# Maxout as (a+b)/2 + |a−b|/2 in a fused attention and maxout kernel

**Chip, cores, metric.** One core of one Trainium2 chip. Times are device microseconds (us) of one execution, as medians of several runs; the span of a profile is the time from the first to the last instruction of the one profiled execution, some 2 us less.

## The reference

Eight batches of block-causal attention (8 heads, 576 positions, head size 64, blocks of 64), whose output is x with 4608 tokens of 512, and then a maxout layer:

```python
attn_out = softmax(masked(q k^T / 8)) v          # per batch and head
x  = attn_out.transpose(0, 2, 1, 3).reshape(4608, 512)
h1 = x @ w1                                      # 512 x 1024
h2 = x @ w2
g  = maximum(h1, h2)
out = g @ w_out                                  # 1024 x 512
```

## The kernel before

The program is one list of instructions in an order chosen by hand: attention goes two head pairs at a time, and matmuls of the maxout layer ("units", one `yield` for each matmul) fill the gaps that attention leaves on TensorE. `fill(n)` takes such matmuls to the worth of n of 512 columns (one of 256 columns counts half). The transposed x lies whole in one SBUF tile, `xT`. The parts that matter:

```python
xT = ring.tile([P, NDM, NTOK + BLK], BF16, name="xT")
w1_sb = wpool.tile([P, NDM, d_ff], BF16, name="w1_sb")
w2_sb = wpool.tile([P, NDM, d_ff], BF16, name="w2_sb")
...
def load_w(f0, fw, which=(0, 1)):            # fp32 in HBM, bf16 in SBUF: the DMA casts
    for i in which:
        dst, src = ((w1_sb, w1r), (w2_sb, w2r))[i]
        nc.gpsimd.dma_start(out=dst[:, :, f0:f0 + fw], in_=src[:, :, f0:f0 + fw])
...
def h_unit(i, f):                            # 128 columns of h, up to 512 tokens
    ...
    for w_sb in (w1_sb, w2_sb):
        pt = ps_m.tile([P, SPAN], FP32, name="ps_h", tag="m")
        for c in range(NDM):                 # NDM = 4
            nc.tensor.matmul(pt[:, :w], w_sb[:, c, ...], xT[:, c, t0:t0 + w], ...)
            if c == NDM - 1:
                if not ph:
                    nc.vector.tensor_copy(out=h1[:, :w], in_=pt[:, :w])
                else:
                    nc.vector.tensor_max(g[:, f, m:m + w], h1[:, :w], pt[:, :w])
                ...
            yield

def y_unit(i, s):                            # 128 tokens of the output
    for f in range(NFF):                     # NFF = 8
        nc.tensor.matmul(py[:], g[:, f, ...], wo_sb[:, f, :], ...)
        ...

def x_out(g, t0=0, t1=NCH, copies=(dve, dve)):   # context -> transposed x
    ...                                          # transposes on TensorE into pe, po
    copies[0](out=dst[:, :, :, 0], in_=pe[:])    # dst is a part of xT
    copies[1](out=dst[:, :, :n_odd, 1], in_=po[:])
```

The start of the schedule (cut): the first two pairs' scores, then `av(0, [0, 1])`, and so on to `x_out(0, 0, 2, (act, act))`, which writes the first piece of xT with ACT, then `x_out(1, 0, 2)` with VectorE, then the first `fill(2)`. The masks of the attention weights (`masks_q`), the loads of v and the casts of q and k are GpSimd's, in program order.

The softmax here doesn't subtract the row's maximum and nothing guards it: scores larger than these inputs give would overflow.

Of the kernel before, what the change touches and what calls it, by code (L numbers as in the profile page):

```python
# [8 lines left out]
FP32 = mybir.dt.float32  # L9
BF16 = mybir.dt.bfloat16  # L10
# [4 lines left out]
def kernel(  # L15
# [10 lines left out]
    nc = tc.nc  # L26

    B, H, S, D = q.shape
    P = 128
# [3 lines left out]
    d_model = H * D  # L33
    d_ff = moe_w1.shape[1]
    NDM = d_model // P
    NFF = d_ff // P
    NTOK = B * S
# [44 lines left out]
    xpool = ctx.enter_context(tc.tile_pool(name="xp", bufs=3))  # L82
    raw = ctx.enter_context(tc.tile_pool(name="raw", bufs=4))
    qkn = ctx.enter_context(tc.tile_pool(name="qkn", bufs=2))
    h1_pool = ctx.enter_context(tc.tile_pool(name="h1", bufs=3))
    g_pool = ctx.enter_context(tc.tile_pool(name="g", bufs=2))
    y_pool = ctx.enter_context(tc.tile_pool(name="y", bufs=4))
    ps_s = ctx.enter_context(tc.tile_pool(name="ps_s", bufs=2, space=bass.MemoryType.PSUM))
# [9 lines left out]
    vv_r = [ring.tile([P, NCH, H, D + 1], BF16, name=f"vv{r}") for r in range(NV)]  # L98
    aT_r = [ring.tile([P, 2, AW + APAD], BF16, name=f"aT{r}") for r in range(NA)]
    xT = ring.tile([P, NDM, NTOK + BLK], BF16, name="xT")  # L100
    w1_sb = wpool.tile([P, NDM, d_ff], BF16, name="w1_sb")
    w2_sb = wpool.tile([P, NDM, d_ff], BF16, name="w2_sb")
    wo_sb = wpool.tile([P, NFF, d_model], BF16, name="wo_sb")
    ident = wpool.tile([P, P], BF16, name="ident")

# [35 lines left out]
    w2r = moe_w2.rearrange("(c p) f -> p c f", p=P)  # L141
    wor = moe_w_out.rearrange("(c p) f -> p c f", p=P)

    def load_w(f0, fw, which=(0, 1)):
        for i in which:
            dst, src = ((w1_sb, w1r), (w2_sb, w2r))[i]
            nc.gpsimd.dma_start(out=dst[:, :, f0:f0 + fw], in_=src[:, :, f0:f0 + fw])

    def load_wo(c0, n):
        nc.gpsimd.dma_start(out=wo_sb[:, c0:c0 + n, :], in_=wor[:, c0:c0 + n, :])  # L150
# [11 lines left out]
    load_qk(2, (SP, None))  # L162
    make_identity(nc, ident)
    for r in range(NV):
        nc.vector.memset(vv_r[r][:, :, :, D:D + 1], 1.0)
        nc.vector.memset(vv_r[r][:BLK, NCH - 1, :, :], 0.0)
    for r in range(NA):
        nc.vector.memset(aT_r[r][:, :, AW:], 0.0)
# [3 lines left out]
    cast("k", 0, ((act, 0, 5), (dve, 5, RPP)))  # L172
    for c in range(2):
        load_v(0, c)
    load_w(0, 256, (0,))
    cast("q", 1, ((pool, 7, RPP),))
    cast("k", 1, ((pool, 0, 7),))
    load_w(0, 256, (1,))
    load_qk(2, (None, SP), gated=True)


    done_tokens = [0]
    g_tiles = {}

    def h_unit(i, f):
        if f == 0:
            g_tiles[i] = g_pool.tile([P, NFF, SPAN + BLK], BF16, name="g")
            if carry[i]:
                end = carry[i - 1] + spans[i - 1][1]
                nc.gpsimd.tensor_copy(  # L190
                    out=g_tiles[i][:, :, :carry[i]],
                    in_=g_tiles[i - 1][:, :, end - carry[i]:end])
        g = g_tiles[i]
        t0, w = spans[i]
        m = carry[i]
        ph = []
        for w_sb in (w1_sb, w2_sb):
            pt = ps_m.tile([P, SPAN], FP32, name="ps_h", tag="m")
            for c in range(NDM):
                nc.tensor.matmul(  # L200
                    pt[:, :w], w_sb[:, c, f * P:(f + 1) * P], xT[:, c, t0:t0 + w],
                    start=(c == 0), stop=(c == NDM - 1),
                )
                if c == NDM - 1:
                    if not ph:
                        h1 = h1_pool.tile([P, SPAN], BF16, name="h1")
                        nc.vector.tensor_copy(out=h1[:, :w], in_=pt[:, :w])  # L207
                    else:
                        nc.vector.tensor_max(g[:, f, m:m + w], h1[:, :w], pt[:, :w])  # L209
                    ph.append(pt)  # L210
                yield

    def y_unit(i, s):
        g = g_tiles[i]
        t0 = spans[i][0] - carry[i] + s * P
        py = ps_m.tile([P, d_model], FP32, name="ps_y", tag="m")
        for f in range(NFF):
            nc.tensor.matmul(  # L218
                py[:], g[:, f, s * P:(s + 1) * P], wo_sb[:, f, :],
                start=(f == 0), stop=(f == NFF - 1),  # L220
            )
            if f == NFF - 1:
                y = y_pool.tile([P, d_model], FP32, name="y")
                (dve if i < 2 else act)(out=y[:], in_=py[:])  # L224
                nc.sync.dma_start(out=out[t0:t0 + P, :], in_=y[:])
            yield

    def y_last(i, s):
        g = g_tiles[i]
        t0 = spans[i][0] - carry[i] + s * P  # L230
        for m, w, copy, queue in ((0, 256, act, SP), (256, P, dve, SP), (384, P, act, ACT)):
            py = ps_m.tile([P, w], FP32, name="ps_y", tag="m")
            for f in range(NFF):
                nc.tensor.matmul(  # L234
                    py[:], g[:, f, s * P:(s + 1) * P], wo_sb[:, f, m:m + w],
                    start=(f == 0), stop=(f == NFF - 1),
                )
                if f == NFF - 1:
                    y = y_pool.tile([P, w], FP32, name="yl")
                    copy(out=y[:], in_=py[:])  # L240
                    queue.dma_start(out=out[t0:t0 + P, m:m + w], in_=y[:])
                yield


    units = []

    def plan():
        def h(i, f):
            t0, w = spans[i]
            units.append((h_unit(i, f), t0 + w, w / SPAN, 2 * NDM))  # L250

        def y(i, s, last=False):
            t0, w = spans[i]
            if last:
                units.append((y_last(i, s), t0 + w, 0.333, 3 * NFF))
            else:
                units.append((y_unit(i, s), t0 + w, 1.0, NFF))

        for i in range(NSPAN):
            for f in range(NFF):  # L260
                h(i, f)
                if i > 2 and f % 2 == 0 and f // 2 < tiles[i - 1]:
                    y(i - 1, f // 2)
            if i == 1:
                for j in range(2):
                    for s in range(tiles[j]):
                        y(j, s)
        n = tiles[-1]
        for s in range(n):
            y(NSPAN - 1, s, s == n - 1)  # L270
# [13 lines left out]
    def fill(n):  # L284
        while n > 0 and at[0] < len(steps) and steps[at[0]][1] <= done_tokens[0]:
            u, _, cost = steps[at[0]]
            next(u)
            n -= cost
            at[0] += 1
# [74 lines left out]
    def burst_p(p):  # L364
        burst(p, ((0, 0, QCUT), (1, P, QCUT - P)), 0)
# [4 lines left out]
    def burst_q2(p):  # L370
        burst(p, ((1, 448, P), (2, QCUT, 320), (4, 512, BLK)), 896)
# [8 lines left out]
    def masks_q(p, eng=None):  # L380
        for a in (1024, 1408):
            mask(p, a, eng)
# [34 lines left out]
    def av(p, ts):  # L417
        b, hp = divmod(p, HP)
        vv = vv_r[b % NV]
        a = aT_r[p % NA]  # L420
        n = len(ts)
        h0 = hp // 2 * 4 + hp % 2
        if p % 2 == 0 and ts[0] == 0:
            xps[p // 2] = xpool.tile([P, NCH, 2, 2, D], BF16, name="xp")
        xp = xps[p // 2]
        po = ps_m.tile([P, n, 2, D + 1], FP32, name="ps_o", tag="m")
        n_mm = 2 * sum(t + 1 for t in ts)
        mm = 0
        for gi, t in enumerate(ts):
            for hh in range(2):  # L430
                for c in range(t + 1):
                    a0 = a_col(p, c, t)
                    nc.tensor.matmul(  # L433
                        po[:, gi, hh, :], a[:, hh, a0:a0 + P], vv[:, c, h0 + 2 * hh, :],
                        start=(mm == 0), stop=(mm == n_mm - 1),
                    )
                    mm += 1
        rec = small.tile([P, 3, 2, 1], FP32, name="rec")
        nc.vector.reciprocal(rec[:, :n, :, 0], po[:, :, :, D])  # L439
        nc.vector.tensor_mul(  # L440
            xp[:, ts[0]:ts[0] + n, :, p % 2], po[:, :, :, :D],
            rec[:, :n].to_broadcast([P, n, 2, D]),
        )
# [26 lines left out]

    def fill_of(g):
        if g == NG - 1:
            return 54
        left = 5 - g if g < 5 else 2 - (g - 5) % 2
        return -(-max(0, ready() - KEEP) // left)

# [44 lines left out]
    masks_p(1)  # L521
    for c in range(2, NCH):
        load_v(0, c)
    load_w(256, 256)
    cq = transposes("q", 1, (dve, dve))
    burst_q1(0)
    ck = transposes("k", 1, (dve, dve))
# [2 lines left out]
        ck((i,), LOW)  # L530
    cq((0,), HIGH, act)
    cq((1,), HIGH, act)
    load_w(512, 512)
    warm_up(3)
    burst_p(2)
    ck((0,), HIGH, dve)
# [1 line left out]
    av(0, [0, 1])  # L538
    warm_up(2)
    burst_p(3)  # L540
    av(1, [0, 1])
    masks_p(2, nc.vector)
    burst_q3(0)
    masks_p(3, nc.vector)
    burst_q2(0)
    av(2, [0, 1])
    warm_up(2)
    x_out(0, 0, 2, (act, act))
# [8 lines left out]
    warm_up(2)  # L557
    burst_q3(1)
    masks_q(1)
    for c in range(3):  # L560
        load_v(1, c)
    fill(2)
    load_qk(3, (SP, SP), gated=True)
    burst_q1(2)
    transposes("q", 2, (dve, act))()
    fill(3)
    burst_q2(2)
    av(0, [2, 3, 4])
    fill(1)
    burst_q3(2)  # L570
    masks_q(2)
    for c in range(3, NCH):
# [14 lines left out]
    cast("q", 3, ((pool, 0, RPP),))  # L587
    cast("k", 3, ((pool, 0, RPP),))
    load_qk(4, (SP, SP), gated=True)
    load_wo(0, 4)  # L590
    load_wo(4, 4)
    fill(3)

    x_due = []
# [35 lines left out]
    for p in range(NPAIR - LAG, NPAIR):  # L630
        if x_due:
            x_out(x_due.pop())
        av_with(p, 5)
        fill(11)
    x_out(NG - 1)
    fill(len(steps))

# [35 lines left out]
```

## Time and profile before

| | before |
|---|---|
| time, median of the 4 runs beside the result (range) | 282.98 us (282.7 to 285.0) |
| span of the profiled run, mean granted clock | 281.0 us, 1.00 |
| TensorE busy | 96% |
| steady part: time for two head pairs and 256 tokens of maxout | 15.0 us |

The page's slices of the span (40 of 7.0 us, busy tenths of TensorE, then its granted clock in tenths) show no hole:

```profile
PE   8699999999999999999999999999999999999995
...
PEclk9999999999999999999999999999999999999999
```

The evictions of h that the change touches, from the groups by form (count, busy us, mean ns):

```profile
L207 DVE CAST h<-ps_h 128x512 bf16<-128x512 f32 x56 | 38.7, 691 | 20.1 <-PE ps_h L200 18.4
L209 DVE TENSOR_TENSOR g<-h,ps_h 128x512 bf16<-128x512 bf16 x56 | 38.4, 686 | 9.1 <-PE ps_h L200 9.1
```

Both kinds of eviction cost the same, and VectorE waits for TensorE in front of them, not the other way round. (The trace of before lacks some 45 matmul records: 3208 matmuls against 3253 weight loads in the busy line below, so TensorE's sums of before are a little low.)

### The profile page before, as it was taken

How to read it: one execution, taken by the hardware profiler on the slowest of the kernel's cores; microseconds unless marked ns; L12 is line 12 of the kernel's file. 1: busy time of each engine (PE TensorE's matmuls, PEld its weight loads, DVE VectorE, ACT ScalarE, POOL GpSimd, SP SyncE). 2: the span in 40 equal slices, each digit the busy share in tenths (PEclk: the TensorE clock that was granted, in tenths of full speed). 3: DMA queues.
4: the chain of work that ended last, by engine and by line, in shares of the span. 5: the costliest groups of instructions: out<-in, count | busy, mean ns of one | idle time of the engine just before them, and what ended most of it. 6: DMA issues, size and time to landing. Idle time of an engine off the chain costs nothing.

```text
span 281.0 us, 7771 instructions
## 1 busy us (share of the span) xinstructions
PE 269.6 (96%) x3208; PEld 151.4 (54%) x3253; DVE 185.1 (66%) x387; ACT 140.8 (50%) x198; POOL 108.3 (39%) x272
## 2 busy tenths in 40 slices
PE   8699999999999999999999999999999999999995
PEld 2356767655556455555555554646454644444543
DVE  5867779668887666767767676757655766455530
ACT  3796577667565565555648375564653000100112
POOL 2996456764754625254343715372120000000000
PEclk9999999999999999999999999999999999999999
DMA  7999999989924993579266875175301111011114
GB/s 259 265 222 224 177 230 274 251 136 203 214 25 160 141 181 63 193 77 244 49 208 70 213 86 184 62 79 45 66 14 40 51 59 42 37 75 40 72 41 149
DMA packets 55940, 36.68 MB, mean 131 GB/s; under 512 B 38752, under 2 KB 43232, under 8 KB 55904
## 3 DMA queue, kind: packets, MB, share of 16 engines
q0 software_dynamic: 41728, 7.87, 34.7%
q1 hardware_dynamic: 13760, 27.66, 29.0%
q10 hardware_dynamic: 416, 0.66, 0.7%
q8 instruction: 25, 0.41, 0.6%
q14 instruction: 11, 0.09, 0.1%
HBM read 34.60 MB, written 9.44 MB: 157 GB/s over the span
## 4 chain that ended last, share of the span: by engine, by line
PE 94%; DVE 2%; ACT 2%; issue 2%; ACTq 0%
PE ps_h L200 43%; PE ps_y L218 22%; PE ps_o L433 11%; PE ps_s L325 8%; PE ps_w L295 3%; PE ps_qT L306 2%; PE ps_xe L455 2%; PE ps_kT L306 2%; ACT aT L349 1%; PE ps_s L343 1%; PE ps_y L234 1%; DVE kT L314 0%; DVE g L209 0%; DVE qn L131 0%; PE ps_xo L457 0%
## 5 line engine op out<-in xcount | busy, mean ns | idle before, releaser
L200 PE MATMUL ps_h<-xT,w_sb 128*128 128x512 bf16 (+3 forms) x605 | 136.2, 357 | 1.7 <-issue 0.3
L349 ACT ACTIVATE aT<-ps_s 128x1024 bf16<-128x1024 f32 (+2 forms) x100 | 96.1, 996 | 16.6 <-PE ps_s L325 15.5
L200 PEld LDWEIGHTS <-w_sb 128*128 128x128 bf16 x640 | 57.8, 98 | 57.4 <-issue 8.1
L207 DVE CAST h<-ps_h 128x512 bf16<-128x512 f32 (+3 forms) x80 | 51.0, 637 | 29.0 <-PE ps_h L200 26.6
L218 PE MATMUL ps_y<-wo_sb,g 128*128 128x512 bf16 x273 | 65.5, 379 | 2.1 <-PE ps_s L325 1.3
L354 POOL MEMSET aT<- 64x128 bf16 x124 | 22.5, 200 | 93.2 <-ACT aT L349 91.7
L209 DVE TENSOR_TENSOR g<-h,ps_h 128x512 bf16<-128x512 bf16 (+3 forms) x80 | 50.6, 632 | 11.8 <-PE ps_h L200 10.1
L224 ACT COPY y<-ps_y 128x512 f32<-128x512 f32 x31 | 18.1, 585 | 70.3 <-PE ps_y L218 56.5
L433 PEld LDWEIGHTS <-aT 128*128 128x128 bf16 x960 | 37.2, 98 | 13.5 <-issue 0.8
L218 PEld LDWEIGHTS <-g 128*128 128x128 bf16 x280 | 26.7, 98 | 30.4 <-issue 1.1
L433 PE MATMUL ps_o<-vv,aT 128*128 128x65 bf16 x960 | 39.8, 194 | 0.0
L135 POOL DMA_DIRECT2D vv<-in_v_dram x40 | 33.7, 847 | 0.5
L325 PE MATMUL ps_s<-qT,kT 64*128 64x64 bf16 (+6 forms) x344 | 31.6, 279 | 1.6 <-ACT kT L314 0.7
L440 DVE TENSOR_TENSOR xp<-ps_o,rec 128x256 bf16<-128x256 f32 (+1 forms) x64 | 31.4, 491 | 2.2
L439 DVE RECIPROCAL rec<-ps_o 128x4 f32<-128x4 f32 (+1 forms) x64 | 12.0, 188 | 21.6 <-PE ps_o L433 20.0
L314 ACT COPY qT<-ps_qT 128x576 bf16<-128x576 bf16 (+1 forms) x17 | 10.3, 614 | 29.4 <-PE ps_qT L306 29.4
L190 POOL COPY g<-g 128x512 bf16<-128x512 bf16 x8 | 4.9, 613 | 38.3 <-DVE g L209 38.2
L131 POOL CAST qn<-qraw 128x1152 bf16<-128x1152 f32 (+1 forms) x16 | 16.9, 1058 | 6.4 <-DMA qraw<-in_q_dram 6.3
L131 POOL CAST kn<-kraw 128x1152 bf16<-128x1152 f32 (+1 forms) x15 | 17.1, 1140 | 5.1 <-DMA kraw<-in_k_dram 2.6
L460 DVE COPY xT<-ps_xe 128x640 bf16<-128x640 bf16 (+2 forms) x17 | 7.9, 463 | 16.1 <-PE ps_xe L455 14.9
L314 ACT COPY kT<-ps_kT 128x576 bf16<-128x576 bf16 x15 | 9.6, 638 | 15.0 <-PE ps_kT L306 15.0
L325 PEld LDWEIGHTS <-kT 64*128 64x128 bf16 x344 | 13.2, 95 | 6.8 <-issue 3.0
(46 smaller groups left out, 145.5 us busy)
## 6 DMA issues: line engine op xcount, KB each, us to landing
qraw<-in_q_dram SPq DMA_DIRECT2D x16, 576.0 KB, 4.1
out_dram<-y SPq DMA_DIRECT2D x35, 256.0 KB, 2.1
kraw<-in_k_dram SPq DMA_DIRECT2D x15, 576.0 KB, 5.5
vv<-in_v_dram POOLq DMA_DIRECT2D x32, 128.0 KB, 5.4
w_sb<-in_moe_w_dram POOLq DMA_DIRECT2D x4, 256.0 KB, 6.5
w_sb<-in_moe_w_dram POOLq DMA_DIRECT2D x2, 512.0 KB, 10.9
wo_sb<-in_moe_w_out_dram POOLq DMA_DIRECT2D x2, 512.0 KB, 11.9
kraw<-in_k_dram ACTq DMA_DIRECT2D x1, 576.0 KB, 5.4
```

What stands on the lines that cost most here:

```text
L131: copy(out=n[:, j0:j1], in_=t[:, j0:j1])
L135: nc.gpsimd.dma_start(out=vv_r[b % NV][P - rows:, c, :, :D], in_=v[b, :, c * P:c * P + rows, :].rearrange("h p d -> p h d"),)
L200: nc.tensor.matmul(pt[:, :w], w_sb[:, c, f * P:(f + 1) * P], xT[:, c, t0:t0 + w], start=(c == 0), stop=(c == NDM - 1),)
L207: nc.vector.tensor_copy(out=h1[:, :w], in_=pt[:, :w])
L209: nc.vector.tensor_max(g[:, f, m:m + w], h1[:, :w], pt[:, :w])
L218: nc.tensor.matmul(py[:], g[:, f, s * P:(s + 1) * P], wo_sb[:, f, :], start=(f == 0), stop=(f == NFF - 1),)
L314: (copy or copies[i])(out=t[:, p0 * RPP:p1 * RPP].rearrange("q (p j) -> q p j", j=RPP), in_=pts[i][:, :, p0:p1].rearrange("q j p -> q p j"),)
L325: nc.tensor.matmul(ps[:, hh, col:col + w], kT[r, k0:k0 + P], qT[r, q0:q0 + w], start=True, stop=True,)
L349: nc.scalar.activation(out=aT_r[p % NA][:, :, a0:a0 + w], in_=ps[:, :, :w], func=AF.Exp, scale=scale,)
L354: (eng or nc.gpsimd).memset(aT_r[p % NA][BLK:, :, a0:a0 + BLK], 0.0)
L433: nc.tensor.matmul(po[:, gi, hh, :], a[:, hh, a0:a0 + P], vv[:, c, h0 + 2 * hh, :], start=(mm == 0), stop=(mm == n_mm - 1),)
L440: nc.vector.tensor_mul(xp[:, ts[0]:ts[0] + n, :, p % 2], po[:, :, :, :D], rec[:, :n].to_broadcast([P, n, 2, D]),)
```

## The change

max(a, b) = (a+b)/2 + |a−b|/2, so out = ½ [ |x(w1−w2)| w_out + x ((w1+w2) w_out) ]. One h product instead of two, with |·| as its eviction; M = (w1+w2) w_out is made once; each output tile takes four more matmuls, x M. The ½ goes into attention's normalisation (the ones column of v becomes 2). To form w1−w2 and w1+w2 in fp32, w1 and w2 are now loaded as fp32 in four chunks of 256 columns, through four slots in the part of xT that is written last; the sum is written beside them.

```diff
-    w1_sb = wpool.tile([P, NDM, d_ff], BF16, name="w1_sb")
-    w2_sb = wpool.tile([P, NDM, d_ff], BF16, name="w2_sb")
+    d_sb = wpool.tile([P, NDM, d_ff], BF16, name="d_sb")
+    sT_sb = wpool.tile([P, NFF, d_model], BF16, name="sT_sb")
+    m_sb = wpool.tile([P, NDM, d_model], BF16, name="m_sb")
...
+    spare = xT[:, :, NTOK - 8 * WB - d_ff:NTOK]
+    w_slots = [spare[:, :, n * 2 * WB:(n + 1) * 2 * WB].bitcast(FP32) for n in range(4)]
+    s_sb = spare[:, :, 8 * WB:8 * WB + d_ff]
...
+    def load_w(j, which=(0, 1)):
+        for i in which:
+            w_raws[j, i] = t = w_slots[2 * (j % 2) + i]
+            nc.gpsimd.dma_start(out=t, in_=(w1r, w2r)[i][:, :, j * WB:(j + 1) * WB])
+    def combine_w(j):
+        fs = slice(j * WB, (j + 1) * WB)
+        nc.vector.tensor_sub(d_sb[:, :, fs], w_raws[j, 0], w_raws[j, 1])
+        nc.gpsimd.tensor_add(s_sb[:, :, fs], w_raws[j, 0], w_raws[j, 1])
...
-        nc.vector.memset(vv_r[r][:, :, :, D:D + 1], 1.0)
+        nc.vector.memset(vv_r[r][:, :, :, D:D + 1], 2.0)
...  h_unit: one product, evicted by
+        nc.vector.tensor_reduce(out=out, in_=in_.unsqueeze(2), op=max, axis=X,
+            apply_absolute_value=True)
...  new units: 32 transposes of s_sb into sT_sb, and M = sT_sb x wo_sb (32 matmuls)
...  y_unit: four terms (xT, m_sb) ahead of the eight (g, wo_sb)
...  schedule of the start: combine_w(0), load_w(2) after burst_p(3); combine_w(1), load_w(3)
...  before av(2, [0, 1]); combine_w(2) after masks_q(1); combine_w(3) after av(0, [2, 3, 4]);
...  load_wo behind load_w(3); the first fillers fill(2), fill(3), fill(1) become 4, 4 and 2
```

More of the change, by code (lines that the diff above doesn't have):

```diff
@@ L84 @@
     qkn = ctx.enter_context(tc.tile_pool(name="qkn", bufs=2))
-    h1_pool = ctx.enter_context(tc.tile_pool(name="h1", bufs=3))
     g_pool = ctx.enter_context(tc.tile_pool(name="g", bufs=2))
@@ L142 @@
     wor = moe_w_out.rearrange("(c p) f -> p c f", p=P)
-    def load_w(f0, fw, which=(0, 1)):
-        for i in which:
-            dst, src = ((w1_sb, w1r), (w2_sb, w2r))[i]
-            nc.gpsimd.dma_start(out=dst[:, :, f0:f0 + fw], in_=src[:, :, f0:f0 + fw])
+    WB = 256
+    w_raws = {}
+    spare = xT[:, :, NTOK - 8 * WB - d_ff:NTOK]
+    w_slots = [spare[:, :, n * 2 * WB:(n + 1) * 2 * WB].bitcast(FP32) for n in range(4)]
+    s_sb = spare[:, :, 8 * WB:8 * WB + d_ff]
+    def load_w(j, which=(0, 1)):
+        for i in which:
+            w_raws[j, i] = t = w_slots[2 * (j % 2) + i]
[4 more added lines that the diff above has]
+        nc.gpsimd.tensor_add(s_sb[:, :, fs], w_raws[j, 0], w_raws[j, 1])
     def load_wo(c0, n):
@@ L174 @@
         load_v(0, c)
-    load_w(0, 256, (0,))
+    load_w(0, (0,))
     cast("q", 1, ((pool, 7, RPP),))
     cast("k", 1, ((pool, 0, 7),))
-    load_w(0, 256, (1,))
+    load_w(0, (1,))
     load_qk(2, (None, SP), gated=True)
@@ L183, with ABS @@
     g_tiles = {}
+    def ABS(out, in_):
+        nc.vector.tensor_reduce(
+            out=out, in_=in_.unsqueeze(2), op=mybir.AluOpType.max,
+            axis=mybir.AxisListType.X, apply_absolute_value=True)
     def h_unit(i, f):
@@ L195, in h_unit, with sT_unit, m_unit @@
         m = carry[i]
-        ph = []
-        for w_sb in (w1_sb, w2_sb):
-            pt = ps_m.tile([P, SPAN], FP32, name="ps_h", tag="m")
-            for c in range(NDM):
-                nc.tensor.matmul(
-                    pt[:, :w], w_sb[:, c, f * P:(f + 1) * P], xT[:, c, t0:t0 + w],
-                    start=(c == 0), stop=(c == NDM - 1),
-                )
-                if c == NDM - 1:
-                    if not ph:
-                        h1 = h1_pool.tile([P, SPAN], BF16, name="h1")
-                        nc.vector.tensor_copy(out=h1[:, :w], in_=pt[:, :w])
-                    else:
-                        nc.vector.tensor_max(g[:, f, m:m + w], h1[:, :w], pt[:, :w])
-                    ph.append(pt)
+        pt = ps_m.tile([P, SPAN], FP32, name="ps_h", tag="m")
+        for c in range(NDM):
+            nc.tensor.matmul(
+                pt[:, :w], d_sb[:, c, f * P:(f + 1) * P], xT[:, c, t0:t0 + w],
+                start=(c == 0), stop=(c == NDM - 1),
+            )
+            if c == NDM - 1:
+                ABS(g[:, f, m:m + w], pt[:, :w])
+            yield
+    def sT_unit(j):
+        pt = ps_m.tile([P, 2, NDM, P], BF16, name="ps_sT", tag="m")
+        for i in range(2):
+            f = 2 * j + i
+            for c in range(NDM):
+                nc.tensor.transpose(pt[:, i, c, :], s_sb[:, c, f * P:(f + 1) * P], ident[:])
+                if i == 1 and c == NDM - 1:
+                    (dve if j % 2 else act)(
+                        out=sT_sb[:, 2 * j:2 * j + 2, :],
+                        in_=pt.rearrange("p i c d -> p i (c d)"))
                 yield
-    def y_unit(i, s):
-        g = g_tiles[i]
-        t0 = spans[i][0] - carry[i] + s * P
-        py = ps_m.tile([P, d_model], FP32, name="ps_y", tag="m")
+    def m_unit(c):
+        pt = ps_m.tile([P, d_model], FP32, name="ps_M", tag="m")
         for f in range(NFF):
             nc.tensor.matmul(
-                py[:], g[:, f, s * P:(s + 1) * P], wo_sb[:, f, :],
+                pt[:], sT_sb[:, f, c * P:(c + 1) * P], wo_sb[:, f, :],
                 start=(f == 0), stop=(f == NFF - 1),
@@ L222, in y_unit, with y_terms @@
             if f == NFF - 1:
+                (act, dve)[c % 2](out=m_sb[:, c, :], in_=pt[:])
+            yield
+    def y_terms(i, s):
+        g = g_tiles[i]
+        t0 = spans[i][0] - carry[i] + s * P
+        return [(xT[:, c, t0:t0 + P], m_sb[:, c]) for c in range(NDM)] + [
+            (g[:, f, s * P:(s + 1) * P], wo_sb[:, f]) for f in range(NFF)]
+    def y_unit(i, s):
+        t0 = spans[i][0] - carry[i] + s * P
+        py = ps_m.tile([P, d_model], FP32, name="ps_y", tag="m")
+        terms = y_terms(i, s)
+        for n, (lhs, rhs) in enumerate(terms):
+            nc.tensor.matmul(
+                py[:], lhs, rhs, start=(n == 0), stop=(n == len(terms) - 1),
+            )
+            if n == len(terms) - 1:
                 y = y_pool.tile([P, d_model], FP32, name="y")
@@ L228, in y_last @@
     def y_last(i, s):
-        g = g_tiles[i]
         t0 = spans[i][0] - carry[i] + s * P
@@ L232, in y_last @@
             py = ps_m.tile([P, w], FP32, name="ps_y", tag="m")
-            for f in range(NFF):
+            terms = y_terms(i, s)
+            for n, (lhs, rhs) in enumerate(terms):
                 nc.tensor.matmul(
-                    py[:], g[:, f, s * P:(s + 1) * P], wo_sb[:, f, m:m + w],
-                    start=(f == 0), stop=(f == NFF - 1),
+                    py[:], lhs, rhs[:, m:m + w], start=(n == 0), stop=(n == len(terms) - 1),
                 )
-                if f == NFF - 1:
+                if n == len(terms) - 1:
                     y = y_pool.tile([P, w], FP32, name="yl")
@@ L245 @@
     units = []
+    NY = NDM + NFF
     def plan():
@@ L249, in h @@
             t0, w = spans[i]
-            units.append((h_unit(i, f), t0 + w, w / SPAN, 2 * NDM))
+            units.append((h_unit(i, f), t0 + w, w / SPAN, NDM))
         def y(i, s, last=False):
@@ L254, in y @@
             if last:
-                units.append((y_last(i, s), t0 + w, 0.333, 3 * NFF))
+                units.append((y_last(i, s), t0 + w, 0.333, 3 * NY))
             else:
-                units.append((y_unit(i, s), t0 + w, 1.0, NFF))
+                units.append((y_unit(i, s), t0 + w, 1.0, NY))
         for i in range(NSPAN):
@@ L261, in plan @@
                 h(i, f)
+                if i == 0 and f % 2 == 1:
+                    units.append((sT_unit(f // 2), 0, 0.3, 2 * NDM))
                 if i > 2 and f % 2 == 0 and f // 2 < tiles[i - 1]:
@@ L264, in plan @@
             if i == 1:
+                for c in range(NDM):
+                    units.append((m_unit(c), 0, 1.0, NFF))
                 for j in range(2):
@@ L472, in fill_of @@
         if g == NG - 1:
-            return 54
+            return 45
         left = 5 - g if g < 5 else 2 - (g - 5) % 2
@@ L523 @@
         load_v(0, c)
-    load_w(256, 256)
+    load_w(1)
     cq = transposes("q", 1, (dve, dve))
@@ L532 @@
     cq((1,), HIGH, act)
-    load_w(512, 512)
     warm_up(3)
@@ L540 @@
     burst_p(3)
+    combine_w(0)
+    load_w(2)
     av(1, [0, 1])
@@ L545 @@
     burst_q2(0)
+    combine_w(1)
+    load_w(3)
+    load_wo(0, 4)
+    load_wo(4, 4)
     av(2, [0, 1])
@@ L559 @@
     masks_q(1)
+    combine_w(2)
     for c in range(3):
         load_v(1, c)
-    fill(2)
+    fill(4)
     load_qk(3, (SP, SP), gated=True)
@@ L565 @@
     transposes("q", 2, (dve, act))()
-    fill(3)
+    fill(4)
     burst_q2(2)
     av(0, [2, 3, 4])
-    fill(1)
+    combine_w(3)
+    fill(2)
     burst_q3(2)
@@ L589 @@
     load_qk(4, (SP, SP), gated=True)
-    load_wo(0, 4)
-    load_wo(4, 4)
     fill(3)
@@ L633 @@
         av_with(p, 5)
-        fill(11)
+        fill(9)
     x_out(NG - 1)
```

## The prediction

> **What bounds the kernel now.** I read the page's busy line first, then the chain that ended last, then the windows of the steady part, then the timeline of the first 30 us.
>
> ```profile
> PE 269.6 (96%) x3208; PEld 151.4 (54%) x3253; DVE 185.1 (66%) x387; ACT 140.8 (50%) x198; POOL 108.3 (39%) x272
> ...
> PE 94%; DVE 2%; ACT 2%; issue 2%; ACTq 0%
> PE ps_h L200 43%; PE ps_y L218 22%; PE ps_o L433 11%; PE ps_s L325 8%; PE ps_w L295 3%; PE ps_qT L306 2%; PE ps_xe L455 2%; PE ps_kT L306 2%; ACT aT L349 1%; PE ps_s L343 1%; PE ps_y L234 1%; DVE kT L314 0%; DVE g L209 0%; DVE qn L131 0%; PE ps_xo L457 0%
> ```
>
> The span is 281.0 us (the quoted time of 282.94 is about 1.9 above it). TensorE is busy 96% of it, and 94% of the chain is TensorE: it is the bound, with the two products h = x w1, x w2 (L200) at 43% and y = g w_out (L218) at 22%. Busy alone would not show this, since matmul ends are modelled; the chain does. The chain in order of time gives the price of one matmul in a dense stretch:
>
> ```profile
> 245.14 3.45 PE ps_h L200 x16
> 248.59 1.73 PE ps_y L218 x8
> ```
>
> 3.45/16 = 0.216 us for 512 columns. The steady part repeats every 15 us (two head pairs), and there every other engine has room:
>
> ```profile
> 105.00:120.00 15.00, 14.74 (x188) 8.26 (x190) 10.21 (x20) 8.60 (x13) 5.57 (x16) 1.00 0.41 120
> 120.00:135.00 15.00, 14.74 (x188) 8.27 (x190) 10.21 (x20) 8.61 (x13) 7.72 (x18) 1.00 0.90 151
> ```
>
> (columns: PE, PEld, DVE, ACT, POOL busy, clock, DMA share, GB/s.) DVE is at 10.2 of 15, ACT at 8.6. So matmul columns taken away there come off the time. The start is different: it is a chain of loads, casts and small steps. The lines of it that I shall need, from the timeline:
>
> ```profile
> 14.04 3.01 POOL L147 DMA_DIRECT2D w_sb<-in_moe_w_dram  x4
> ...
> 16.44 0.37 ACT L460 COPY xT<-ps_xe 128x256 bf16<-128x256 bf16 x1
> ...
> 17.06 2.32 ACT L349 ACTIVATE aT<-ps_s 128x1024 bf16<-128x1024 f32 x3
> 17.09 1.14 POOL L131 CAST qn<-qraw 128x1152 bf16<-128x1152 f32 x1
> ...
> 18.66 0.61 PE L200 MATMUL ps_h<-xT,w_sb 128*128 128x256 bf16 x4
> ```
>
> The first piece of x is copied by ACT at 16.44, done by 17.09; three exponentials follow, and the first h matmul starts at 18.66. From 20 us on TensorE is over 96% busy. The weight loads at 14.04 are four issues of about 0.78 us each. For the first two of them (the tile view of the weights, 14.5 to 15.2 us) the time from issue to landing is:
>
> ```profile
> DMA to landing us min/median/max: 7.0/7.3/7.6
> ```
>
> so the second lands at 14.82 + 7.6 = 22.4 us. The first two weight loads (issued at 8.07 and 10.13) took 5.9 us each.
>
> **What the Trainium skill says.** (1) "TensorE: Matmul & The Clock Gate", back-to-back issue gap: N/2.4 + 2.5 ns, so 216 ns for 512 columns and 56 for 128. The trace agrees (0.216). Its Part 1 says that after an idle window of about 3.4 us the array runs at half rate until it has been busy as long. The trace shows only the start: the first weight loads stand 0.43 us apart, twice 0.216. (2) "VectorE: DVE Perf Modes", the perf-mode tier table: tensor_reduce has no fast mode, and fp32 in PSUM gets none either. So the absolute value (a tensor_reduce over groups of one element) should cost what the cast from PSUM does, 0.69 us for 128x512; no run of before has one, so an added cost for each output is possible. (3) "GPSIMD Engine Reference", section 3: an fp32 add of two tensors of 2048 elements takes 4497 ns on GpSimd and 2293 on VectorE. Half of that for 1024 elements: an estimate of 2.3 us and 1.2 us. The trace has no GpSimd add of two inputs; its casts of one input run at 1.15 us for 1152 elements, about twice as fast for each element, which fits.
>
> **The change part by part, on TensorE.**
> Removed: one of the two h products, 320 matmuls. Half of the 43.4% of 281 us on the chain is 61 us; by columns, 4608 x 32 / 512 = 288 full matmuls x 0.216 = 62. I take 61.5.
> Added: four more terms in every y tile, 36 tiles x 4 x 0.216 = 31.1. The product M = (w1+w2) w_out: 32 x 0.216 = 6.9. The transposes of w1+w2: 32 of 128 columns, some 0.06 each, 1.9.
> Net: 61.5 - 31.1 - 6.9 - 1.9 = 21.6 us less TensorE work. VectorE loses the other 80 evictions (101.6 us for both kinds, about 50 left), so the steady part, 15.0 - 1.9 = 13.1 us by the same sums, stays TensorE-bound: DVE goes to about 7, ACT stays at 8.6. Were that all, the time would be 261.
>
> **The same change in the first 40 us.** Now w1 and w2 come in as fp32, in four chunks of 256 columns, two chunks in flight, staged in the part of the x tile that is not yet written. VectorE forms w1-w2 and GpSimd w1+w2 chunk by chunk, and a slot is loaded again only after both. I listed the changed kernel's instructions by engine with the semaphores they wait on. Three things stand there:
> - GpSimd's first add waits for the loads of chunk 0 and of chunk 1; its second add waits for chunk 2 as well as 1. The sum is written beside the slots, in the same tile, and is treated as touching all of them.
> - ACT's first copy into the x tile (16.44 before) and VectorE's of the second piece wait for the last loads of all four chunks. The columns do not overlap; the rows' address ranges do.
> - In GpSimd's order, the cast of the third q, the masks and the next v loads stand behind all this.
> So nothing of the projection starts until: chunk 1 landed, 22.4; add, 2.4 with its semaphore; load of chunk 2; add, 2.4; load of chunk 3. For a pair of loads I take 5.6 us from the second issue, a little under the 5.9 of the first chunk since the queues are then empty, plus 0.8 for the first issue: 6.4. Sum: 22.4 + 2.4 + 6.4 + 2.4 + 6.4 = 40.0 us for the last landing. ACT's copies end at 40.7 where they ended at 17.09: 23.6 us later, and the exponentials, the score buffers behind them and the first h matmul move by the same. TensorE idles from about 19 us with a few steps between, so the clock drops, and half rate for about 3.4 us costs some 1.5. GpSimd then does masks, the third add, three v loads (2.6), the fourth add, and only then the masks of the third pair: 40.0 + 4 + 2.3 + 2.7 + 2.4 + 0.4 = about 51.8. They are needed by the context matmuls that stood here:
>
> ```profile
> 25.43 0.88 PE L433 MATMUL ps_o<-vv,aT 128*128 128x65 bf16 x24
> ```
>
> TensorE itself gets there at 25.4 + 23.6 + 1.5 + 0.9 (it has done some transposes of w1+w2 by then) = 51.4, so both meet at about 51.6: 26.2 later than before. Of these, 0.9 is work already counted in the net.
> Sum: 282.9 + 26.2 - 0.9 - 21.6 = 286.6; with a little for evictions of M and of the transposes, 287.
>
> **The rivals.**
> A: the start is not held up, because the loads land fast or the waits are met early; then the time goes to 261 to 265. For it: TensorE's sums are firm, and the author has moved loads to suit. Against it: the waits are in the instruction list, and two rounds of load-then-add in series can't be shorter than two landings.
> B: the start is held up, but less: loads in an empty queue at 4 us as for the q rows (median 4.1 for 576 KB, from another queue), and adds at 1.3 us: 22.4 + 1.4 + 4.8 + 1.4 + 4.8 = 34.8, and the time is some 281.
> C: VectorE becomes the bound because a reduction over one element costs two or more cycles for each output: 1.2 us for 512. In the steady part DVE would be at about 9.5 of 13, so this shows little; at 3 cycles it would, some 5 us or more on top, 292.
> D: TensorE waits more in the steady part, as there are fewer filler matmuls between the scores and the exponentials. Two exponentials take 2.1 us, and the filler, context and transposes between two pairs of score tiles still make about 4.7 us; I expect nothing of it, at most 2 us.
>
> **Range and chances.** The net on TensorE is good to 1.5 us. The hold-up is the soft term: three landings and two adds, each good to 1 us or so, and what GpSimd's order adds after them: plus or minus 5 together. So 287, and 280 to 293 holds it 8 times in 10. Faster by over 2% (under 277.3) needs the hold-up to be under 17 us: 0.07. Slower by over 2% (over 288.6) needs only 2 us more than my sum: 0.35. Within 2%: 0.58.
>
> **What would show each step.** Right: one weight matrix's h matmuls on the chain with about 61 us and y with about 93; the steady period near 13.1 us; TensorE's slices from about the third to the sixth nearly empty, with a clock below full; the first ACT copy into x waiting on a weight load and ending near 40.7; GpSimd adds of about 2.3 us; absolute values of 0.69 us. Wrong: a first h matmul before 33 us or after 48 (a landing or an add mis-sized); a period of 14 or more (rivals C, D); TensorE waiting for VectorE in the second half.

## The result, and the profile after

| | before | after |
|---|---|---|
| median (range) | 282.98 us (282.7 to 285.0, 4 runs) | **291.07 us** (290.52 to 292.51, 4 runs) |
| ratio, 95% interval | 1 | 1.028, 1.024 to 1.033: slower |
| span, mean clock of the profiled run | 281.0 us, 1.00 | 289.0 us, 0.952 |

A ratio here and below is the mean time of one kernel's fast runs over the mean of the other's fast runs of the same rounds, so it isn't quite the ratio of the medians.

The page of the changed kernel, its busy line, slices, clock and chain:

```profile
PE 255.5 (88%) x3149; PEld 140.4 (49%) x3149; DVE 142.9 (49%) x315; ACT 143.8 (50%) x202; POOL 119.0 (41%) x278
...
PE   8730209999999898999999999999999999999995
...
PEclk9985558999999999999999999999999999999999
...
PE 77%; DMA 9%; POOL 8%; ACT 3%; issue 1%; DVE 1%; POOLq 0%; ACTq 0%
```

TensorE has less to do, 255.5 us instead of 269.6 (and instead of a little more, for the missing records), but slices four to six are nearly empty at half clock (slice three is 0.3 busy at 0.8). The chain, 94% TensorE before, now has 9% of transfers and 8% of GpSimd. In order of time the first 55 us of the chain read like a list of the hold-up (start us, us, what):

```profile
14.79 9.48 DMA xT<-in_moe_w_dram
24.49 2.35 POOL xT L159
27.12 0.77 POOL xT L154
27.89 5.39 DMA xT<-in_moe_w_dram
33.45 2.34 POOL xT L159
36.08 0.77 POOL xT L154
36.84 5.35 DMA xT<-in_moe_w_dram
...
45.51 2.35 POOL xT L159
47.85 2.63 POOL vv L135 x3
50.95 2.35 POOL xT L159
53.61 0.84 PE ps_o L475 x22
```

L154 is a load of a weight chunk, L159 the fp32 sum on GpSimd. Load, add, issue, load, add, issue, load: each waits for the one before. What starts once the last chunk is in, from the timeline:

```profile
42.29 0.37 ACT L502 COPY xT<-ps_xe 128x256 bf16<-128x256 bf16 x1 [25.89 <-DMA xT<-in_moe_w_dram]
...
44.19 1.89 PE L215 MATMUL ps_h<-xT,d_sb 128*128 128x256 bf16 x8
...
53.36 0.34 POOL L396 MEMSET aT<- 64x128 bf16 x2
...
53.61 0.84 PE L475 MATMUL ps_o<-vv,aT 128*128 128x65 bf16 x22 [0.17 <-POOL aT L396]
```

ACT stood idle for 25.89 us, waiting for a weight load, before its first copy into xT (at 16.44 before). TensorE's third context product of 24 matmuls, at 25.43 before, comes at 53.61, behind GpSimd's masks (its first two matmuls ran at 53.20 already). The sizes of the new instructions, from the groups by form:

```profile
L198 DVE TENSOR_REDUCE g<-ps_h 128x512 bf16<-128x512 f32 x56 | 38.4, 689 | 29.8 <-PE ps_h L215 29.8
L159 POOL TENSOR_TENSOR xT<-xT 128x1024 bf16<-128x1024 f32 x4 | 9.4, 2342 | 14.1 <-DMA xT<-in_moe_w_dram 13.7 <-DVE d_sb L158 0.3
```

The absolute value costs 689 ns, no more than the cast it replaces (691). In the steady part the chain shows the period: the same group of ten output matmuls returns after 13.35 us (15.0 before):

```profile
120.54 2.16 PE ps_y L257 x10
...
133.89 2.16 PE ps_y L257 x10
```

So the change does what it is meant to once the start is over. Taking the third context product as the mark: up to it the changed kernel is 53.61 − 25.43 = 28.2 us later; from it to the end it needs 289.0 − 53.6 = 235.4 us, where before needs 281.0 − 25.4 = 255.6, so it wins back 20.2. Net 8.0, the difference of the spans.

Why does a copy into the first columns of xT wait for a load into its last columns? The waits in the compiled program of the changed kernel say what each instruction is made to wait for (an excerpt of the instruction list, which isn't kept with the runs; DMASW are semaphores of loads that GpSimd issued):

```
ACT   first copy into xT   waits: DMASW3, DMASW2, DMASW4, DMASW1 (loads of chunks 2 and 3), PE
DVE   first copy into xT   waits: the same
POOL  first add (chunk 0)  waits: DMASW2,3 (chunk 0), DMASW0,7 (chunk 1), DVE
POOL  second add (chunk 1) waits: also chunk 2's loads
```

The trace agrees: the first add starts at 24.49, when chunk 1 has landed (24.27), and the second at 33.45, when chunk 2 has (33.28). The columns don't overlap, but all views are strided views of one tile, and the program's waits are set as if they did. The theory for the experiments: these waits inside one tile, on top of a chain of three landings, make the hold-up. Rivals: GpSimd's add of 2.34 us is too slow (VectorE needs 1.22 for the same shape); or the clock at half rate is what costs.

### The profile page after: what moved, and what is told of

It reads as the page before. It is cut to its first block, busy times and chain, and to the rows that moved or that the text cites. A ratio compares the mean times of both kernels' runs of the same rounds, so it can differ in the third digit from the quotient of the medians.

```text
span 289.0 us, 7516 instructions
## 1 busy us (share of the span) xinstructions
PE 255.5 (88%) x3149; PEld 140.4 (49%) x3149; DVE 142.9 (49%) x315; ACT 143.8 (50%) x202; POOL 119.0 (41%) x278
## 4 chain that ended last, share of the span: by engine, by line
PE 77%; DMA 9%; POOL 8%; ACT 3%; issue 1%; DVE 1%; POOLq 0%; ACTq 0%
PE ps_y L257 32%; PE ps_h L215 21%; PE ps_o L475 9%; DMA xT<-in_moe_w_dram 7%; PE ps_s L367 6%; POOL xT L159 3%; ACT aT L391 3%; POOL vv L135 2%; DMA qraw<-in_q_dram 2%; PE ps_M L238 2%; PE ps_kT L348 2%; PE ps_qT L348 2%; PE ps_xe L497 2%; POOL xT L154 1%; PE ps_y L272 1%
## 5 line engine op out<-in xcount | busy, mean ns | idle before, releaser
L215 PE MATMUL ps_h<-xT,d_sb 128*128 128x512 bf16 (+3 forms) x320 | 73.1, 362 | 0.4 <-DVE xT L503 0.2
L198 DVE TENSOR_REDUCE g<-ps_h 128x512 bf16<-128x512 f32 (+3 forms) x80 | 50.6, 636 | 43.5 <-PE ps_h L215 42.6
L257 PE MATMUL ps_y<-wo_sb,g 128*128 128x512 bf16 x280 | 69.9, 379 | 0.0
L215 PEld LDWEIGHTS <-d_sb 128*128 128x128 bf16 x320 | 28.9, 99 | 28.6 <-issue 4.2
L257 PEld LDWEIGHTS <-g 128*128 128x128 bf16 x280 | 25.7, 98 | 30.2 <-issue 2.8
L257 PE MATMUL ps_y<-m_sb,xT 128*128 128x512 bf16 x140 | 38.0, 380 | 0.2 <-DVE m_sb L243 0.2
L367 PE MATMUL ps_s<-qT,kT 64*128 64x64 bf16 (+6 forms) x344 | 32.3, 284 | 3.2 <-ACT aT L447 1.6
L337 PE MATMUL ps_w<-zeros 128*128 128x512 bf16 x29 | 10.2, 493 | 23.7 <-DVE xT L502 12.2
L257 PEld LDWEIGHTS <-xT 128*128 128x128 bf16 x140 | 12.9, 98 | 15.8 <-issue 2.6
```

The source lines that it names most:

```text
L198: nc.vector.tensor_reduce(out=out, in_=in_.unsqueeze(2), op=mybir.AluOpType.max, axis=mybir.AxisListType.X, apply_absolute_value=True)
L215: nc.tensor.matmul(pt[:, :w], d_sb[:, c, f * P:(f + 1) * P], xT[:, c, t0:t0 + w], start=(c == 0), stop=(c == NDM - 1),)
L257: nc.tensor.matmul(py[:], lhs, rhs, start=(n == 0), stop=(n == len(terms) - 1),)
L367: nc.tensor.matmul(ps[:, hh, col:col + w], kT[r, k0:k0 + P], qT[r, q0:q0 + w], start=True, stop=True,)
```

## The experiments

All are edits of the changed kernel unless said, all gave correct results, and each was timed against before on the same chip (before: 283.11 us in the first set of four, 282.90 without its slow run, which the ratios leave out; 282.94 in the second set of two, 282.89 for the last).

### 1. The sum in a tile of its own

```diff
-    s_sb = spare[:, :, 8 * WB:8 * WB + d_ff]
+    s_sb = wpool.tile([P, NDM, d_ff], BF16, name="s_sb")
...
-                    y = y_pool.tile([P, w], FP32, name="yl")
+                    y = y_pool.tile([P, w], FP32, name="yl", bufs=3)      # to fit
```

> The sum w1+w2 in a tile of its own: the compiled waits of the GpSimd adds on later chunks' loads go, those of the first x copies on all loads stay. Theory (the start is held up by waits on address ranges that do not overlap): add 0 starts at about 16 us instead of 24.5, chunk 2 is asked for at about 19, add 1 starts when chunk 1 has landed (24.4), chunk 3 is asked for at 27 and lands near 33 instead of 42.2; all after it is 9 us earlier: time 282 (280 to 284). Rival (the hold-up is the two staging slots alone, the waits cost nothing): no change, 291.

Measured: 288.00 us (287.14 to 288.85, 4 runs), ratio 1.018 (1.015 to 1.021). A gain of 3 us; the size was missed. The timeline shows why:

```profile
17.70 3.36 POOL L159 TENSOR_TENSOR s_sb<-xT 128x1024 bf16<-128x1024 f32 x1 [2.18 <-DMA xT<-in_moe_w_dram]
...
35.58 0.37 ACT L502 COPY xT<-ps_xe 128x256 bf16<-128x256 bf16 x1 [19.14 <-DMA xT<-in_moe_w_dram]
...
43.09 4.22 DVE L158 TENSOR_TENSOR d_sb<-xT 128x1024 bf16<-128x1024 f32 x1
```

The adds no longer wait for the next chunk (the first starts at 17.70 instead of 24.49), and ACT's copy goes 6.7 us earlier, 35.58 instead of 42.29. But the add now starts 0.07 us after VectorE's subtraction of the same chunk and takes 3.36 us instead of 2.34; the false wait had kept the two apart. Later VectorE's last subtraction takes 4.22 us instead of 1.22 while GpSimd adds from 43.83 to 46.21, and what stands behind it on VectorE is late: TensorE waits 3.14 us for the next eviction of h (at 47.69). The Trainium skill's page "SBUF — State Buffer", section "Who interferes with whom", says that a VectorE instruction with two SBUF inputs contends with a GpSimd instruction that reads SBUF. Its section "SBUF: two separate sides" says that whichever of the two starts first holds the shared ports for its whole instruction and that "the other fully blocks". The first case agrees: 3.36 − 2.34 = 1.02, most of the 1.23 us of the subtraction that came first. So part of what the wait took away was given back as contention between the two engines; in the end the normalisation that follows the third context product is 2.7 us earlier (51.75 instead of 54.49), which is about the gain.

### 2. The slots out of xT

The slots go to the tile of w_out, which is loaded after the last combination, and to a tile of their own; the sum stays in xT.

```diff
-    w_slots = [spare[:, :, n * 2 * WB:(n + 1) * 2 * WB].bitcast(FP32) for n in range(4)]
+    stage = wpool.tile([P, 2 * NDM, 2 * WB], BF16, name="stage")
+    w_slots = [t[:, i * NDM:(i + 1) * NDM, :].bitcast(FP32) for t in (wo_sb, stage) for i in range(2)]
...  load_wo(0, 4), load_wo(4, 4) moved behind combine_w(3); yl bufs=3, to fit
```

> The staging slots moved out of the x tile (half in the not yet loaded w_out tile, half in a tile of their own), order of work kept, w_out loaded after the last add. Theory: no x copy waits on a weight load, first ACT copy near 19 us, no 20 us hole in TensorE; what is left is GpSimd's order (adds, then cast of the third q, then masks of the third pair near 41 us instead of 53.4): 12 us earlier, time 279 (276 to 282). Rival (fp32 loads through the DMA queue are the hold-up, 4 MB instead of 2 MB written): no change of more than 2 us.

Measured: 281.34 us (280.81 to 282.12, 4 runs), ratio 0.995 (0.992 to 0.998). The expectation held: the same arithmetic and the same loads, without a load into the tile that the copies write, take 9.7 us less than the change as given (9.5 by the ratios, 1.028 and 0.995, since the two were timed on different occasions).

```profile
20.91 0.37 ACT L503 COPY xT<-ps_xe 128x256 bf16<-128x256 bf16 x1 [4.81 <-PE ps_xe L498]
...
28.62 1.89 PE L216 MATMUL ps_h<-xT,d_sb 128*128 128x256 bf16 x8
...
42.06 0.34 POOL L397 MEMSET aT<- 64x128 bf16 x2
```

The copy waits for TensorE alone; the first h matmuls come at 28.62 instead of 44.19. But the masks of the third pair come at 42.06 (53.36 in the change as given): in GpSimd's order they still stand behind four fp32 sums and the loads that feed them, and TensorE waits 3.17 us for them (at 42.31). That part of the hold-up is left, and the contention of run 1 is here too (its first two adds take 3.36 and 3.38 us). The clock was still 0.50 from 20 to 30 us.

### 3. The sum on VectorE

```diff
-        nc.gpsimd.tensor_add(s_sb[:, :, fs], w_raws[j, 0], w_raws[j, 1])
+        nc.vector.tensor_add(s_sb[:, :, fs], w_raws[j, 0], w_raws[j, 1])
```

> w1+w2 on VectorE (1.2 us for each chunk) instead of GpSimd (2.34 us), staging and waits as in the changed kernel. Theory: the chain of two loads and two adds gets shorter by 2 x 1.1 us and GpSimd's two later adds leave the masks' way: last landing near 39.7, time 288.5 (286.5 to 290). Rival (slow GpSimd adds are the main cause): 280 or less.

Measured: 291.39 us (290.05 to 292.82, 4 runs), ratio 1.030 (1.026 to 1.034): no change against 291.07. Not confirmed. The adds took 1.23 us instead of 2.34, yet the copy goes only 1.4 us earlier (40.92 instead of 42.29):

```profile
40.92 0.37 ACT L502 COPY xT<-ps_xe 128x256 bf16<-128x256 bf16 x1 [24.22 <-DMA xT<-in_moe_w_dram]
```

and VectorE's own order then stands in the way: the last subtraction and sum (49.34 to 51.8) precede the copies of k, and the normalisation after the third context product comes at 55.68, 1.2 us later than in the change as given. So GpSimd's slowness at adding isn't the main cause: the rival (280 or less) fell.

### 4 and 6. TensorE kept warm

First both in one, which was badly designed:

```diff
     x_out(0, 0, 2, (act, act)) ; av(3, [0, 1]) ; burst_q1(1)
...
+    warm_up(50)
     x_out(1, 0, 2)
-    warm_up(2)
+    warm_up(64)
```

> 114 more idle-time matmuls while TensorE waits, so its clock does not drop. Theory: the next gate is GpSimd's masks of the third pair at 53.4 us, so a full clock after 43 us gains nothing: 290.5 to 291.5, and the wait ahead of those context matmuls grows from 0.2 to about 1.5 us. Rival (the low clock costs time of its own): 289.3 or less.

Measured: 303.66 us (303.51 to 304.01, 4 runs), ratio 1.073. The 64 dummy matmuls did not fill the gap: their PSUM buffer comes free only with the copies that wait, so they ran after it, 13.97 us on the path.

```profile
44.03 13.97 PE L337 MATMUL ps_w<-zeros 128*128 128x512 bf16 x64
```

It says nothing on the clock. In its place, the first 50 alone, which can run in the gap:

> As the changed kernel with 50 idle-time matmuls, now all placed where they run inside the wait (30 to 43 us), so the clock is full when the x copies come. Theory: the masks of the third pair at about 53.4 us are the next gate, so the time stays 290.5 to 291.5 and only the wait ahead of those context matmuls grows. Rival (the low clock costs its own 1.5 us): 289.8 or less.

Measured: 291.78 us (290.50 to 292.63, 4 runs), ratio 1.031 (1.028 to 1.034), as expected of no gain; the mean clock rose from 0.952 to 0.971. What the warmer array won turned into a longer wait of the same instruction as before, now 0.83 us for GpSimd's masks instead of 0.17:

```profile
54.42 0.83 PE L475 MATMUL ps_o<-vv,aT 128*128 128x65 bf16 x22 [0.83 <-POOL aT L396]
```

In this profile the copy itself came 1.2 us later (43.46 instead of 42.29); from the copy to this context product it is 10.96 us, where the change as given took 11.32. So the low clock cost at most some 0.4 us of its own here: GpSimd was the next gate.

### 5. The same algebra on bf16 loads

w1 and w2 are loaded as before, through the DMA that casts, into tiles of their own; VectorE makes the difference into `d_sb` and the sum in place of w2; the transposed sum takes the place of w1.

```diff
-    sT_sb = wpool.tile([P, NFF, d_model], BF16, name="sT_sb")
+    w1_sb = wpool.tile([P, NDM, d_ff], BF16, name="w1_sb")
+    w2_sb = wpool.tile([P, NDM, d_ff], BF16, name="w2_sb")
+    s_sb = w2_sb
+    sT_sb = w1_sb.rearrange("p c f -> p (c f)").rearrange("p (f d) -> p f d", d=d_model)
...
-        nc.vector.tensor_sub(d_sb[:, :, fs], w_raws[j, 0], w_raws[j, 1])
-        nc.gpsimd.tensor_add(s_sb[:, :, fs], w_raws[j, 0], w_raws[j, 1])
+        nc.vector.tensor_sub(d_sb[:, :, fs], w1_sb[:, :, fs], w2_sb[:, :, fs])
+        nc.vector.tensor_add(w2_sb[:, :, fs], w1_sb[:, :, fs], w2_sb[:, :, fs])
...  loads in the places and sizes of before; combine_w(0, 256), (256, 256), (512, 512) ahead of
...  their first use; transposes of the sum in span 1; w_out asked for where before asks for it;
...  fillers of the start cut to 11 in all (before 15, the change as given 19); yl bufs=3, to fit
```

> The same algebra (same products, same y tiles, same M), but w1 and w2 come in as in the kernel before (cast to bf16 by the DMA, into tiles of their own, asked for at the same places), and both the difference and the sum are made by VectorE from bf16; GpSimd keeps its old order. Theory (TensorE's saving of 21.6 us is real and only the start took it back): first h matmul near 19 us, no hole, no low clock; 283 - 21.6 + 2 (waits on ACT as in the changed kernel) + 1 (VectorE's extra 6 us at the start) = 264 to 266, range 262 to 268. Rival (the algebra itself, with its M and its reductions, brings less): 270 or more.

Measured: 273.27 us (271.74 to 274.87, 6 runs), ratio 0.965 (0.962 to 0.968). It beats both kernels, but by 8 us less than expected. TensorE now waits in the start for the new steps (engine, tile, line, what it waited for: us, times, longest):

```profile
PE ps_h L211 <- DVE d_sb L154: 3.6, 3, 1.8
...
PE ps_M L234 <- DMA wo_sb<-in_moe_w_out_dram: 2.1, 1, 2.1
```

The threshold of the rival (270 or more) was met. But its reason, that the algebra itself brings less, doesn't hold in the steady part: there the group of ten output matmuls returns after 13.35 us here too (103.13 and 116.48). The shortfall is in the start: from 10 to 50 us TensorE is busy 30.0 us, against 37.7 before. And the edit asks for less filler there than before does (11 against 15 matmuls of 512 columns), which the expectation didn't count.

### 7. The last one with another order

The in-place sums are moved to the end of the start's schedule, the differences are made in pieces of 256 columns, and w_out is asked for before the first filler, 11.8 us earlier (22.88 instead of 34.67).

```diff
     def combine_w(f0, fw): ...
         nc.vector.tensor_sub(...)
-        nc.vector.tensor_add(w2_sb[:, :, fs], w1_sb[:, :, fs], w2_sb[:, :, fs])
+    def sum_w(f0, fw): ...                     # the add alone; sum_w(0, 512) and
+        nc.vector.tensor_add(...)              # sum_w(512, 512) around the last fill(3)
...
+    load_wo(0, 4) ; load_wo(4, 4)              # ahead of the first fill(2)
```

> The bf16-load version (273.3 us) with three moves and nothing else: the in-place sums w1+w2 (0.7 + 0.7 + 2.05 us of VectorE) are taken out of the first 35 us and done late, the differences are made in pieces of 256 columns, and w_out is asked for some 8 us earlier. If the bf16-load version lost its time in the start to VectorE's order and to the late w_out (waits of TensorE of 3.6 us on d and 2.1 us on w_out, of some 6.4 us missing there), this takes most of that back: 268 to 270 us, with those two waits under 2 us together. Rival: TensorE's holes of the start come from too few filler matmuls between scores and exponentials (ACT sets the pace), or w_out only moves the queue: then 272 to 274, the waits turning up at ACT. Threshold 271. The result is right in either case.

Measured: 272.93 us (272.45 to 274.60, 6 runs), ratio 0.965 (0.961 to 0.969). The two waits are gone, the time isn't: my theory missed, the rival's range held. The holes are elsewhere, for instance the two of TensorE here, shown with what stood ahead on VectorE:

```profile
22.52 0.69 DVE L154 TENSOR_TENSOR d_sb<-w_sb 128x1024 bf16<-128x1024 bf16 x1 [2.30 <-DMA w_sb<-in_moe_w_dram]
...
23.93 1.48 PE L474 MATMUL ps_o<-vv,aT 128*128 128x65 bf16 x24 [1.70 <-DVE qT L355]
...
33.13 1.83 DVE L158 TENSOR_TENSOR w_sb<-w_sb 128x2048 bf16<-128x2048 bf16 x1
...
35.10 0.56 DVE L481 TENSOR_TENSOR xp<-ps_o,rec 128x384 bf16<-128x384 f32 x1
...
35.71 0.20 PE L496 MATMUL ps_xe<-ident,xp 64*128 64x64 bf16 x1 [1.85 <-DVE xp L481]
```

TensorE waits for ordinary steps of attention, a copy of q and a normalisation, but these are late because of the new steps. The copy (at 23.13) stands behind a difference of the weights, for whose load VectorE sat idle for 2.30 us. The normalisation stands behind the two sums that this run moved: meant to leave the first 35 us, they ran between 31.66 and 34.96 all the same. A third wait, 0.90 us at 28.77, follows another difference that waited 1.45 us for its load. So the run moved the waits and did not take them away, and its theory, that VectorE's order costs the time, isn't refuted by the time alone. ACT, which the rival named, is waited for only once in the start by more than 0.5 us (0.74 us at 48.28), so the rival was right on the time and not on the engine. The windows from 30 to 40 us, before and then this version (busy us of TensorE, weight loads, VectorE, ACT, GpSimd, then clock, DMA share and GB/s):

```profile
30.00:40.00 10.00, 9.94 (x129) 6.64 (x128) 8.15 (x19) 6.45 (x10) 5.84 (x19) 1.00 1.23 167
```

```profile
30.00:40.00 10.00, 7.65 (x88) 5.21 (x85) 7.84 (x16) 3.37 (x5) 3.55 (x9) 0.88 1.24 230
```

Over 10 to 50 us TensorE is busy 31.9 us here against 37.7 before, in part at a lower clock (0.83 to 0.95 from 20 to 50). The three waits sum to 4.45 us; the busy time is 5.8 us smaller. By the trace, then, most of what is missing stands behind the change's own steps on VectorE; no run without them there tests it. What the lighter filler adds (11 matmuls asked for where before asks for 15) is not shown: a run with other filler in that place wasn't made.

## Why the prediction was right, and where it was off

The mechanism held, step by step, and the time (287 predicted, 291.07 measured) lay within the range. The class did not come out as the likeliest: "within 2%" had 0.58, "slower by over 2%" had 0.35, and it was slower by 2.8%. The sum was 4 us short, and two terms of it were mis-sized.

| term | predicted | measured |
|---|---|---|
| chunk 1 landed | 22.4 us | 24.3 (14.79 + 9.48) |
| last landing | 40.0 | 42.2 (36.84 + 5.35) |
| ACT's two copies end | 40.7 | 42.9 |
| third context product | 51.6, both engines meeting | 53.6, waiting 0.17 for GpSimd |
| later than before there | 26.2 | 28.2 |
| won back after it | 21.6 + 0.9 = 22.5 | 20.2 |

- **The hold-up was 2.0 us longer, and nearly all of it is one landing.** I took chunk 1's second load as 7.6 us, the longest of before's two loads at that place. It took 9.48. The two are not the same transfer: before's casts to bf16, after's is fp32 into xT. The later links nearly cancel: from the first issue of a pair to its last landing 6.2 and 6.1 us (27.12 to 33.28, 36.08 to 42.19) where I took 6.4, and from a landing over the add to the next issue 2.8 (24.27 to 27.12, 33.28 to 36.08) where I took 2.4.
- **The gain after it was 2.3 us smaller.** 1.6 of these are two waits of TensorE for ACT, 0.8 each, which before's trace doesn't have; this is rival D, of which I expected "nothing, at most 2 us". The line of the waits in the changed kernel:

```profile
PE ps_s L367 <- ACT aT L447: 1.6, 2, 0.8
```

  The other 0.7 I can't assign: before's sums lack some 45 matmul records. By line the chain has 59.5 us of h (20.6% of 289.0; I said about 61) and 93.1 of y (32.2%; I said about 93).
- **The steady period** is 13.35 us, not 13.1. In one period before does 32 h matmuls and 16 of y, after 16 and 24: eight fewer, 8 x 0.216 = 1.7 us. My 1.9 matches what 61.5 - 31.1 = 30.4 us give over 16 periods, but the 4608 tokens are 18 portions of 256.
- **The price of a matmul**, 0.216 us, was right by the trace. But the section "Back-to-back issue gap" of the Trainium skill's page "TensorE: Matmul & The Clock Gate", which the prediction cites for it, calls the formula that of an isolated matmul and gives about 131 ns as sustained for 512 columns. The chain (16 matmuls in 3.45 us) decides for 216.
- **Rival A and B** (a start held up not at all, or less) fell; the waits that I read from the instruction list were real, and run 2 shows their price by taking the slots out of xT: 9.7 us. **Rival C** fell: 689 ns for the absolute value.
- **The half clock**, which I put at 1.5 us ahead of the third context product, cost at most some 0.4 us of its own (run 6). I had both engines meeting there anyway, so it did not hurt the sum.
- The prediction saw the fp32 sums on GpSimd at 2.3 us as a link of the chain, and so they were (2.34); but run 3 shows that halving that link alone gives nothing, as the work only changes the engine whose order holds up the start.

The split of the hold-up, as far as the runs show it: false waits between parts of xT cost 9.7 us, net of the contention that comes when they go (run 2); with the fp32 staging and GpSimd's sums gone as well, another 8 (run 5, 281.34 to 273.27), which isn't divided further, since run 5 changes loads, engine, order and filler at once. Between the 273 us of runs 5 and 7 and the 261 that TensorE's sums alone give, some 12 us are not recovered; TensorE's smaller busy time from 10 to 50 us (by 5.8 us in run 7) is about half, most of it behind the new steps on VectorE, and the rest stays open.

## What to carry to other kernels

Before work is taken off the busiest engine, ask what the new inputs of the cheaper form need at the start, where that engine isn't the bound: here 20 us were saved on TensorE and 28 us of delay came in ahead of it. Here a staging buffer cut out of a tile that others write put the writers of that tile behind the loads, at 9.7 us; look in the compiled waits, not in the column ranges, for who waits for whom. And a wait removed may have kept two engines apart that slow each other: after taking it away, compare durations as well as start times. And when an engine waits for an ordinary step, look what stands ahead of that step in its engine's order.

## What the Trainium skill lacked or had wrong

- "SBUF — State Buffer", section "SBUF: two separate sides": it says that whichever instruction starts first gets the shared port pair and the other blocks, and gives no durations for a two-input pair. Where VectorE's subtraction was just ahead, GpSimd's add took 3.36 us instead of 2.34, which agrees. So does run 2, where a subtraction that came during an add (33.15 to 35.50) took 2.06 us from 34.52. But in run 1 VectorE's subtraction, recorded from 43.09, took 4.22 us instead of 1.22 though the add is recorded only from 43.83; it ended 1.1 us after the add did (46.21). By the recorded starts it was the first that blocked. What held it from 43.09 to 43.83 stays open; GpSimd was issuing loads of v until 43.77.
- "DMA: Bandwidth & Descriptors", section "Anatomy of one DMA — SWDGE (gpsimd) path": its fit (2.0 us and bytes over 436e3 for each us) gives 3.2 us for a 512 KB load, as an estimate. The eight fp32 loads of the changed kernel, all of 512 KB, took 3.8 to 9.5 us, median 5.5. The one that mis-sized the prediction (9.48 us) was issued while loads of v and its partner of the pair were in flight; whether that is the reason was not tried, and the fit has no term for it. Before, the same loads of v and two more weight loads were in flight there, and the two landings took 7.0 and 7.6 us.
